# Two row tiles centred instead of normalised at the head of a fused attention and feed-forward kernel, with the first loads in another order

## The chip, the cores and the metric

The kernel runs on one core of a Trainium2 chip. The metric is the device time of one execution in microseconds (us). A core has TensorE (PE, matmuls, with weight loads PEld beside them), VectorE (DVE), ScalarE (ACT), GpSimd (POOL) and SyncE (SP, which here only issues DMAs). Each engine executes its own queue in order; waits between engines go by semaphores. PSUM, which matmuls write, has eight banks.

## The reference

A block on x of 2048 rows and 576 columns: layer norm, then a linear attention and a gated feed-forward in parallel, both added to x.

```python
xn = _layernorm(x)                          # (x - mean) / sqrt(var + 1e-5), per row
# A: 32 heads of 18 columns
q, k, v = split(xn @ wqkv)                  # wqkv: 576 x 1728
phi = lambda t: where(t > 0, t + 1, exp(t)) + 1e-6
kv = einsum("bhsd,bhse->bhde", phi(k), v);  z = einsum("bhsd->bhd", phi(k))
o = einsum("bhqd,bhde->bhqe", phi(q), kv) / (einsum("bhqd,bhd->bhq", phi(q), z)[..., None] + 1e-6)
A = o.reshape(B, S, D) @ wo
# B: F = 4608
B = (gelu(xn @ w_gate) * (xn @ w_up)) @ w_down
return x + A + B
```

All tensors are bf16.

## The kernel before

The 2048 rows are 16 tiles of 128 (`n` = 0 to 15) and four chunks of 512 (`sc`, four tiles each). The feed-forward width is 36 slices of 128 (`f`), loaded two at a time as blocks (`load_gu`): a `wg` and a `wu` tile for the first 512 rows of the weights, and for every second block a `wr` tile with the last 64 rows of both.

**The head**, up to about 58 us, prepares everything that needs all rows. For each tile: `x` is loaded, mean and variance come from two bn_stats and an aggregate on DVE, rstd from Ln and Exp on ACT (`ln_rstd`), and the normalised tile `xn` from DVE or ACT as the string `NORM` says (`ln_norm`, L318). A copy of 64 columns on POOL (`x_twin`) pads the tile to 640 columns, so that its last 64 rows stand twice when transposed. The transposed tile `xnT` comes in two ways: tiles 0 to 3 by ten small transposes on PE into PSUM banks 0 and 1 and two copies (ACT and DVE, `tp_copy`), tiles 4 to 15 by a DMA through the crossbar (`dma_transposes`, L346), which SP issues.

Then come the units on PE. A token unit K*n* or Q*n* multiplies tile *n* with the K or Q columns of `wqkv`; a unit g*f* multiplies the first 512 rows with a slice of gate and up. Each is a `_Unit` (L241): two accumulators in two banks, each fed by matmuls of 64 rows at once. In the first part (`rows`) the lower half of the rows works on the first bank and the upper half on the second; then they take turns, for which POOL gives a sign (`swap`), and the second part (`p2`) follows. A `_Token` unit is either read at once for phi (Exp on ACT, a clamp and a combining operation on DVE) or, for the names in `RAW_T`, copied out by ACT (`raw`, L406) and given its phi after 40 us. A unit can begin only when the former owner of its two banks has been read. K and Q of the head take their banks from one ring (`HEAD_T`), the others from another.

The order of PE is written by hand in `line` (L441): two units are open at a time. `t0` to `t3` are the transposes on PE, "." closes the oldest open unit. All other engines, SP's queue among them, are put in order by a planner (`in_order`, L67): every step has an engine, a cost, a rank, what it comes after and a time before which it is not planned; each engine then executes in the planned order. So the constants `X_AT`, `W_AT` and `DMA_FREE` change the order only, they are not waits. The loads at L189 to L207 stand ahead of the planned ones: x of tiles 0 to 3, K's and Q's weights, x of tiles 4 to 9, and block 0 in between. `first_loads` (L539) fixes the order of those that follow on SP. Each DMA signals one of eight semaphores in turn, and a DMA waits at issue until the one that last used its semaphore has landed.

`z_add` sums phi(K) over the tiles on DVE. After the head, `gram` multiplies phi(K) with `xn` on PE, and the rest is steady: gate and up of the remaining slices, the down product and the outputs, chunk by chunk.

Of the kernel before, what the change touches and what calls it, by code (L numbers as in the profile page):

```python
# [14 lines left out]
P = 128  # L15
HP = 64
# [21 lines left out]
NWARM = 43  # L38
# [7 lines left out]
HEAD_T = RAW_T + ("K2",)  # L46
LATER = 40.0

# [38 lines left out]
def kernel(  # L87
# [32 lines left out]
    banks, head_banks = _Ring([0, 1, 4, 5, 6, 7, 2, 3]), _Ring([4, 5, 6, 7, 2, 3])  # L120
# [31 lines left out]
    xn = apool.tile([P, NS, XW], BF16, name="xn")  # L152
    g_sb = apool.tile([P, KT, D], BF16, name="g_sb")
    z_sum = apool.tile([P, D], F32, name="z_sum")
    z_bf = apool.tile([P, D], BF16, name="z_bf")

# [3 lines left out]
    def load_w_main(which):  # L160
        c = slice(which * D, (which + 1) * D)
        nc.sync.dma_start(wqkv_sb[:, 0:4, c], A_wqkv[0:4 * P, c].rearrange("(kt p) c -> p kt c", p=P))

# [30 lines left out]
    load_x(1, 1, nc.scalar)  # L194
    load_w_main(1)
    load_w_last(1, LO)
    load_w_last(1, HI)
    load_x(2, 1)
    load_w_main(0)
    load_x(3, 1)  # L200
    load_w_last(0, LO)
    load_w_last(0, HI)
    load_x(4, 2)
    load_x(6, 2)
    load_gu(0, 0)
    load_gu(0, 1)
    load_x(8, 2)  # L207

    eps_ln = const.tile([P, 1], F32, name="eps_ln")
# [94 lines left out]

    def ln_aggr(n):
        nc.vector.bn_aggr(out=mv[:, n, :], in_=ln_raw[n][:])
# [11 lines left out]
    def ln_norm(n):  # L318
# [4 lines left out]
        else:  # L323
            nc.vector.tensor_scalar(
                out=xn[:, n, :], in0=x_sb[:, n, :], scalar1=mv[:, n, 0:1], scalar2=rstd[:, n:n + 1],
                op0=ALU.subtract, op1=ALU.mult,
# [9 lines left out]
    def transposes(n):  # L336
        for kt in range(KT):
            for b, rows in enumerate((LO, HI)):
                nc.tensor.transpose(tp_bank(b)[:, kt, :], xn[rows, n, kt * P:(kt + 1) * P], ident[rows, rows])

    def tp_copy(n, b):
        copy = nc.vector.tensor_copy if b else nc.scalar.copy
        t0 = n * P + b * HP
        copy(out=xnT[:, :, t0:t0 + HP], in_=tp_bank(b)[:, 0:KT, :])  # L344
# [4 lines left out]
    X_AT = [3.35, 4.40, 7.10, 9.20]  # L349
    W_AT = {"K": 6.00, "Q": 8.80}  # L350
    DMA_FREE = 12.7
# [5 lines left out]
    for n, at in ((4, 10.2), (6, 11.2), (8, 14.5)):  # L357
        step(("x", n), "none", 0.0, 0, [], lambda: None, ready=at)
    for n in range(10, NS, 2):
        load(("x", n), 0.58, 295, 7.0 + 2.5 * (n - 10), [], lambda n=n: load_x(n, 2), ready=6.0)  # L360

    for n in range(NS):
# [3 lines left out]
        x_at = X_AT[n] if n < 4 else 11.5 if n < 8 else 2.1 * both  # L366
        if n < 4:
            step(("twin", n), "POOL", 0.2, first, [], lambda n=n: x_twin(n, 1), ready=x_at)
        elif n == both:
            step(("twin", n), "POOL", 0.25, first, after_x, lambda n=n: x_twin(n, 2), ready=2.6 * n)  # L370
        twin = ("twin", n if n < 4 else both)
        for h in range(2):
            step(("stats", n, h), "DVE", 0.42, first, after_x, lambda n=n, h=h: ln_half(n, h), ready=5.1 if (n, h) == (1, 1) else x_at)
        step(("aggr", n), "DVE", 0.16, first, [("stats", n, 0), ("stats", n, 1)], lambda n=n: ln_aggr(n), tail=0.05)
        if n < 6:
            step(("rstd", n), "ACT", 0.46, first - 2.0 * (n == 3), [("aggr", n)], lambda n=n: ln_rstd(n, 1))
        elif n == both:
            step(("rstd", n), "ACT", 0.46, first, [("aggr", n), ("aggr", n + 1)], lambda n=n: ln_rstd(n, 2))
# [5 lines left out]
        if n < HEAD:  # L384
            step(("norm", n), on, took, first, ready, lambda n=n: ln_norm(n), tail=0.05)
            free = [("xnT", n - 1, i) for i in range(2)] if n else []
            step(("tp", n), "PE", 0.2, 0, [("norm", n)] + free, lambda n=n: transposes(n), tail=0.15)
            for i, copied in enumerate((0.44, 0.30)):
                step(("xnT", n, i), "DVE" if i else "ACT", copied, first, [("tp", n)], lambda n=n, i=i: tp_copy(n, i), tail=0.02)
            steps[("xnT", n)] = _Step("none", 0.0, first, [("xnT", n, 0), ("xnT", n, 1)], lambda: None, 0.0, 0.0)  # L390
        else:
# [3 lines left out]
    class _Token:  # L395

        def __init__(self, kind, n, ring=banks):
# [3 lines left out]
                [ps_all[:, b, :HALF] for b in self.banks], lambda i, rows, kt: xnT[rows, kt, n * P:(n + 1) * P],  # L401
                lambda i, rows, kt: wqkv_sb[rows, kt, self.c + i * HALF:self.c + (i + 1) * HALF], nc.gpsimd, first=range(KT),
            )
            self.acc = ps_all[:, self.banks[0]:self.banks[0] + 2, :HALF]

# [526 lines left out]
```

## Time and profile before

| | us |
|---|---|
| median of 3 runs (range) | 509.65 (509.18 to 510.46) |
| profiled execution | 509.63 |
| its span, first to last instruction | 507.8 |
| first K matmul (K0) | 6.60 |
| first g matmul (g0) | 14.04 |
| first matmul of `gram` | 58.25 |
| granted PE clock, all slices | 0.9 or more |

PE is busy in 99% of the span. The profile's page, its waits, its timeline and the chain of waits are all of this one execution; times in them start at the span's start. In a timeline row the columns are start, length, engine, line, operation, tiles written and read, form, count, and in brackets the engine's idle time just ahead and what ended it. A DMA row gives queue, count, size and the median time from issue to landing.

### The profile page before, as it was taken

The numbers are of one execution on the slowest core, as the hardware profiler recorded it, in microseconds if no ns is written. First come the engines' busy times: TensorE is split into PE (matmuls) and PEld (weight loads), VectorE is DVE, ScalarE is ACT, GpSimd is POOL, SyncE is SP. The second block draws the span as 40 slices with busy tenths as digits, with TensorE's granted clock in tenths as the row PEclk, the third lists the DMA queues.
The fourth block names the chain that finished last, engine by engine and source line by source line (L and its number), as shares of the span: only waits on it lengthen the run. The fifth ranks groups of instructions, "written<-read, shape, count | busy, mean of one in ns | idle before, by whom it ended". The sixth has DMA issues, their size and how long they took to land.

```text
span 507.8 us, 11198 instructions
## 1 busy us (share of the span) xinstructions
PE 502.7 (99%) x4772; PEld 305.6 (60%) x4772; DVE 228.7 (45%) x477; ACT 151.9 (30%) x265; POOL 8.2 (2%) x32
## 2 busy tenths in 40 slices
PE   8999999999999999999999999999999999999997
PEld 7566875446777444445777444445777444445774
DVE  5778966774101665543101665543101665543101
ACT  4888634335000532233000432233000432232000
POOL 2110000000000000000000000000000000000000
PEclk9999999999999999999999999999999999999999
DMA  9999906996200555654000455654000555640000
GB/s 263 239 220 241 266 1 180 248 269 121 71 13 25 145 150 156 176 163 108 12 13 25 142 151 152 179 162 109 14 12 26 144 151 156 175 112 14 13 13 23
DMA packets 113611, 61.58 MB, mean 121 GB/s; under 512 B 23250, under 2 KB 113562, under 8 KB 113562
## 3 DMA queue, kind: packets, MB, share of 16 engines
q1 hardware_dynamic: 113418, 60.72, 46.9%
q8 instruction: 37, 0.61, 0.5%
q10 hardware_dynamic: 144, 0.15, 0.1%
q14 instruction: 12, 0.10, 0.1%
HBM read 53.75 MB, written 2.36 MB: 110 GB/s over the span
## 4 chain that ended last, share of the span: by engine, by line
PE 94%; DVE 3%; DMA 2%; SPq 1%; issue 0%; ACT 0%; DVEq 0%
PE ps_all L252 58%; PE ps_all L847 28%; PE ps_all L558 3%; PE ps_all L852 3%; DVE hT L422 1%; DMA wu<-in_B_w_up_dram 1%; DMA wqkv_sb<-in_A_wqkv_dram 1%; DVE z_sum L529 1%; DVE phi_e L416 0%; PE ps_all L835 0%; PE ps_all L566 0%; DVE pq L422 0%; SPq L158 0%; PE ps_all L585 0%; PE ps_all L787 0%
## 5 line engine op out<-in xcount | busy, mean ns | idle before, releaser
L252 PE MATMUL ps_all<-xnT,wu 64*128 64x512 bf16 x1152 | 272.7, 376 | 0.3 <-DMA wu<-in_B_w_up_dram 0.3
L252 PE MATMUL ps_all<-xnT,wg 64*128 64x512 bf16 x1152 | 272.6, 376 | 0.0
L252 PEld LDWEIGHTS <-wu 64*128 64x128 bf16 x1152 | 107.9, 94 | 68.4 <-DMA wu<-in_B_w_up_dram 0.8
L252 PEld LDWEIGHTS <-wg 64*128 64x128 bf16 x1152 | 108.2, 94 | 65.2
L740 DVE TENSOR_TENSOR hT<-ps_all,gl 128x512 bf16<-128x512 f32 x130 | 89.9, 691 | 104.1 <-ACT gl L739 104.0
L847 PEld LDWEIGHTS <-hT 128*128 128x128 bf16 x1152 | 110.8, 98 | 30.9 <-issue 1.2
L739 ACT ACTIVATE gl<-ps_all 128x512 f32<-128x512 f32 x130 | 77.6, 597 | 164.1 <-PE ps_all L252 163.7
L861 DVE TENSOR_TENSOR res<-ps_all,x_sb 128x288 bf16<-128x288 f32 (+2 forms) x32 | 13.8, 455 | 146.3 <-PE ps_all L852 88.1
L847 PE MATMUL ps_all<-wd_a,hT 128*128 128x288 bf16 (+2 forms) x512 | 68.3, 286 | 0.0
L252 PE MATMUL ps_all<-xnT,wr 64*128 64x512 bf16 x288 | 57.3, 376 | 0.0
L847 PE MATMUL ps_all<-hT 128*128 128x288 bf16 (+2 forms) x384 | 52.4, 286 | 0.0
L761 ACT ACTIVATE gl<-ps_all 128x288 f32<-128x288 f32 x24 | 9.2, 410 | 121.4 <-PE ps_all L252 118.5
L847 PE MATMUL ps_all<-wd_m,hT 128*128 128x288 bf16 (+2 forms) x256 | 36.8, 286 | 0.0
L252 PEld LDWEIGHTS <-xnT 64*128 64x128 bf16 x576 | 32.6, 94 | 6.7 <-ACT xnT L344 0.9
L252 PE MATMUL ps_all<-wqkv_sb,xnT 64*128 64x288 bf16 x360 | 27.8, 283 | 0.7 <-ACT xnT L344 0.3
L252 PEld LDWEIGHTS <-wr 64*128 64x128 bf16 x288 | 15.2, 94 | 16.4
L852 PE MATMUL ps_all<-m_sb,pqT 128*128 128x288 bf16 (+2 forms) x128 | 20.9, 286 | 0.0
L558 PE MATMUL ps_all<-hT,xn 128*128 128x288 bf16 x128 | 16.0, 286 | 0.0
L437 ACT CAST hT<-ps_all 128x1024 bf16<-128x1024 f32 x14 | 14.1, 1010 | 4.0 <-PE ps_all L252 3.8
L558 PEld LDWEIGHTS <-xn 128*128 128x128 bf16 x128 | 12.4, 98 | 3.5 <-issue 0.5
L852 PEld LDWEIGHTS <-pqT 128*128 128x128 bf16 x128 | 12.4, 98 | 3.3
L303 DVE BATCH_NORM_STATS2 stats<-x_sb 128x6 f32<-128x288 bf16 x32 | 12.9, 435 | 2.9 <-DMA x_sb<-in_A_x_dram 2.9
(79 smaller groups left out, 228.4 us busy)
## 6 DMA issues: line engine op xcount, KB each, us to landing
wg<-in_B_w_gate_dram SPq DMA_DIRECT2D x72, 256.0 KB, 3.0
wu<-in_B_w_up_dram SPq DMA_DIRECT2D x72, 256.0 KB, 3.7
wr<-in_B_w_gate_dram SPq DMA_DIRECT2D x36, 64.0 KB, 3.2
wr<-in_B_w_up_dram SPq DMA_DIRECT2D x36, 64.0 KB, 2.9
wd_a<-in_B_w_down_dram SPq DMA_DIRECT2D x4, 576.0 KB, 8.2
out_dram<-res SPq DMA_DIRECT2D x15, 144.0 KB, 1.8
wqkv_sb<-in_A_wqkv_dram SPq DMA_DIRECT2D x3, 576.0 KB, 5.6
x_sb<-in_A_x_dram SPq DMA_DIRECT2D x6, 288.0 KB, 4.3
```

The source lines that it names most:

```text
L252: return nc.tensor.matmul(self.outs[i], lhsT=self.lhs(i, rows, kt), rhs=self.rhs(i, rows, kt), start=start, stop=stop, skip_group_check=True,)
L303: nc.vector.bn_stats(out=ln_raw[n][:, h, :], in_=x_sb[:, n, h * HALF:(h + 1) * HALF])
L422: nc.vector.scalar_tensor_tensor(out=dst[:, self.n, :].rearrange("p (h c) -> p h c", h=2), in0=self.acc, scalar=0.0, in1=self.e[:].rearran ...
L437: nc.scalar.copy(out=hT[:, self.f:self.f + NF + 1:NF, :], in_=ps_all[:, self.two[0]:self.two[0] + 2, :],)
L529: nc.vector.tensor_tensor(out=(z_bf if i == NS - 1 else z_sum)[:], in0=pk[:, z_order[0], :] if i == 1 else z_sum[:], in1=pk[:, z_order[i], :],
L558: nc.tensor.matmul(ps_all[:, two[hf], :HALF], lhsT=xn[:, n, kt * P:(kt + 1) * P], rhs=pk[:, n, hf * HALF:(hf + 1) * HALF], start=(n == 0), ...
L739: nc.scalar.activation(out=gl[:], in_=ps_all[:, b[0], :], func=ACT.Gelu_apprx_tanh)
L740: nc.vector.tensor_tensor(out=hT[:, GUB * k + i, :], in0=ps_all[:, b[1], :], in1=gl[:], op=ALU.mult)
L761: nc.scalar.activation(out=e[:, :HALF], in_=acc, func=ACT.Exp)
L847: nc.tensor.matmul(self.acc(hf), lhsT=hT[:, f, j * P:(j + 1) * P], rhs=wd(f)[:, self.parts[hf]], start=(f == 0 and not paired), stop=False ...
L852: nc.tensor.matmul(self.acc(hf), lhsT=pqT[:, c, self.ts], rhs=m_sb[:, c, self.parts[hf]], start=False, stop=(paired and c == 3), skip_grou ...
L861: nc.vector.tensor_tensor(out=self.res[:, hs], in0=self.acc(hf), in1=x_sb[:, self.n, hs], op=ALU.add)
```

## The change

For tiles 0 and 1 (`CENTRED`), K and Q are computed from the centred tile, x minus mean, and rstd is applied where the unit's result is copied out of PSUM: per row, on ACT for tile 0 and on DVE for tile 1. The tile normalised in full is made later, and its transpose for the g units comes by a crossbar DMA (`xnU`). The statistics of tile 1 are a sum on ACT, a mean on POOL and a squared sum on ACT. rstd of tiles 1 and 2 is one pair of instructions. The transposes of tiles 0, 1 and 2 use different columns of their banks.

Of the loads: Q's main weights come in four quarters (64 rows by 288 columns of each of four blocks), the last 64 rows of K's and of Q's weights as one DMA each into a tile `w_ends`, K's on ACT's queue. Block 0 of gate and up stands right behind x of tile 3; x of tiles 4 to 9 is planned behind it. Q2 moves from the end of `line` to its head, the warm-up on PE is 36 matmuls for 43, and the ring of banks has another order.

```diff
-NWARM = 43
+NWARM = 36
-HEAD_T = RAW_T + ("K2",)
+HEAD_T = RAW_T + ("K2", "Q2")
+CENTRED = (0, 1)
...
-    banks, head_banks = _Ring([0, 1, 4, 5, 6, 7, 2, 3]), _Ring([4, 5, 6, 7, 2, 3])
+    banks, head_banks = _Ring([0, 1, 6, 7, 4, 5, 2, 3]), _Ring([4, 5, 6, 7, 2, 3])
...
+    def load_w_quarters(which, halves):
+        for rows, half in zip((LO, HI), halves):
+            c = which * D + half * HALF
+            view = A_wqkv[0:4 * P, c:c + HALF].rearrange("(kt p) c -> p kt c", p=P)
+            nc.sync.dma_start(wqkv_sb[rows, 0:4, c:c + HALF], view[rows])
+    def load_w_ends(which, on=nc.sync):
+        c = which * D
+        on.dma_start(w_ends[:, which, :], A_wqkv[512:576, c:c + D].rearrange("r (i c) -> i r c", i=2))
...
     load_x(1, 1, nc.scalar)
+    load_w_ends(1, nc.scalar)
     load_w_main(1)
-    load_w_last(1, LO)
-    load_w_last(1, HI)
     load_x(2, 1)
-    load_w_main(0)
+    load_w_quarters(0, (0, 1))
+    load_w_quarters(0, (1, 0))
+    load_w_ends(0)
     load_x(3, 1)
-    load_w_last(0, LO)
-    load_w_last(0, HI)
-    load_x(4, 2)
-    load_x(6, 2)
     load_gu(0, 0)
     load_gu(0, 1)
-    load_x(8, 2)
...
+    def act_sum(n):
+        nc.scalar.activation(out=act_junk[:], in_=x_sb[:, n, 0:D], func=ACT.Copy, accum_out=act_acc[:])
+    def act_mean(n):
+        for out, by in ((mv[:, n, 0:1], 1.0), (act_bias, D ** -0.5)):
+            nc.gpsimd.tensor_scalar(out=out[:], in0=act_acc[:], scalar1=-by / D, scalar2=None, op0=ALU.mult)
+    def act_square(n):
+        nc.scalar.activation(
+            out=act_junk[:], in_=x_sb[:, n, 0:D], func=ACT.Square, bias=act_bias[:], scale=D ** -0.5, accum_out=mv[:, n, 1:2],
+        )
+    def centre(n):
+        nc.vector.tensor_scalar(
+            out=xn[:, n, :], in0=x_sb[:, n, :], scalar1=mv[:, n, 0:1], scalar2=None, op0=ALU.add if n else ALU.subtract,
+        )
...
-        copy(out=xnT[:, :, t0:t0 + HP], in_=tp_bank(b)[:, 0:KT, :])
+        copy(out=(xcT if n in CENTRED else xnT)[:, :, t0:t0 + HP], in_=tp_bank(b)[:, at:at + KT, :])
...
-    for n in range(10, NS, 2):
+    for n in range(4, NS, 2):
         load(("x", n), 0.58, 295, 7.0 + 2.5 * (n - 10), [], lambda n=n: load_x(n, 2), ready=6.0)
...
+            if late:
+                load(("xnU", n), 1.25, 80, first + 2, [("norm", n)], lambda n=n: dma_transposes(n))
...
-            nc.scalar.copy(out=dst, in_=self.acc)
+            if self.n == 0:
+                nc.scalar.activation(out=dst, in_=self.acc, func=ACT.Identity, scale=rstd[:, 0:1])
+            elif self.n == 1:
+                nc.vector.tensor_scalar(out=dst, in0=self.acc, scalar1=rstd[:, self.n:self.n + 1], scalar2=None, op0=ALU.mult)
+            else:
+                nc.scalar.copy(out=dst, in_=self.acc)
...
-    line = ["t0", "K0", "t1", ".", "K1", "Q0", "t2", "Q1", "t3", "K2", "K3", "g0", "g1", "g2", "g3"]
+    line = ["t0", "t1", "K0", "K1", "Q0", "t2", "Q1", "K2", "Q2", "t3", ".", "K3", "g0", "g1", "g2", "g3"]
...
-    line += ["Q2", "Q3"]
+    line += ["Q3"]
...
-            after = [("xnT", m) for m in range(TPC)] + ([("gu", blk, i) for i in range(2)] if blk else [])
+            after = [("xnU" if m in CENTRED else "xnT", m) for m in range(TPC)] + ([("gu", blk, i) for i in range(2)] if blk else [])
...
+        of += [("phi", "K13")] * (i == 8)
...
     first_loads = [
-        ("x", 10), ("xnT", 4), ("gu", 2, 0), ("xnT", 5), ("gu", 2, 1), ("x", 12), ("xnT", 6), ("x", 14), ("xnT", 7),
-        ("gu", 3, 0), ("gu", 3, 1), ("gu", 4, 0),
+        ("xnU", 0), ("x", 4), ("xnU", 1), ("x", 6), ("gu", 1, 0), ("gu", 1, 1), ("x", 8), ("x", 10), ("xnT", 4), ("gu", 2, 0), ("xnT", 5), ("gu", 2, 1), ("x", 12), ("gu", 3, 0), ("xnT", 6), ("gu", 3, 1), ("xnT", 7), ("x", 14), ("gu", 4, 0),
     ]
```

## The prediction

> **What bounds the kernel now.** I read the page first, then who waited for whom on PE, then the chain of waits, then PE's timeline where the chain leaves PE. The page settles the scale: PE is the bound, and only waits that PE meets can be won.
>
> ```profile
> PE 502.7 (99%) x4772; PEld 305.6 (60%) x4772; DVE 228.7 (45%) x477; ACT 151.9 (30%) x265; POOL 8.2 (2%) x32
> PE 94%; DVE 3%; DMA 2%; SPq 1%; issue 0%; ACT 0%; DVEq 0%
> ```
>
> The second line is the chain's share by engine: some 25 of 507.8 us belong to something other than PE, and the chain in order of time says where.
>
> ```profile
> 1.26 4.65 DMA wqkv_sb<-in_A_wqkv_dram
> ...
> 9.38 5.49 DMA wu<-in_B_w_up_dram
> 14.86 0.04 issue
> 14.91 25.64 PE ps_all L252 x271
> ...
> 54.64 0.77 DVE hT L422
> 55.41 0.04 issue
> 55.45 2.87 PE ps_all L252 x44
> ```
>
> Columns are start, length, what. K's weights land at 5.91 (1.26 + 4.65), the first `wu` block at 14.86, and phi of K13 on DVE ends at 55.41; PE continues right after the last two. From 14.91 to 53.9 PE has no gap (38.94 of 38.94 us busy in that window), and after 58 it runs from `gram` on. So the change can win in two places, which PE's timeline shows:
>
> ```profile
> 6.60 0.79 PE L252 MATMUL ps_all<-wqkv_sb,xnT 64*128 64x288 bf16 x10 [0.26 <-ACT xnT L344]
> ...
> 14.04 0.40 PE L252 MATMUL ps_all<-xnT,wr 64*128 64x512 bf16 x2
> 14.26 0.38 PE L252 MATMUL ps_all<-xnT,wg 64*128 64x512 bf16 x1
> 14.91 0.39 PE L252 MATMUL ps_all<-xnT,wu 64*128 64x512 bf16 x1 [0.27 <-DMA wu<-in_B_w_up_dram]
> ...
> 53.87 1.42 PE L252 MATMUL ps_all<-wqkv_sb,xnT 64*128 64x288 bf16 x18
> 55.45 2.87 PE L252 MATMUL ps_all<-wqkv_sb,xnT 64*128 64x288 bf16 x44 [0.16 <-DVE hT L422]
> ```
>
> Work in these units: two 512-wide matmuls of a pair of row halves start 0.216 us apart, so a g unit (9 pairs) is 1.94; a K and a g follow each other every 3.045 (24.44, 27.49, 30.53 in the timeline), so a token unit is 1.105 (its first five pairs 0.61, its last four 0.49). g0 starts at 14.04, but its second `wu` matmul runs at 14.91 where 14.26 was due: 0.65 lost, as if g0 had begun at 14.69. At the tail 53.87 + 1.105 = 54.98, and PE goes on at 55.45: 0.47 lost to phi of K13.
>
> **The change part by part.**
>
> *Start.* Without rstd on the way, `centre` of tile 0 follows its aggregate (4.42): 4.45 to 4.90, by the 0.45 of the norm at 5.08. Transposes come 0.2 later, 5.1 for 5.74, and the warm-up is cut to suit: 7 of 43 matmuls at 4.75/43 = 0.11 each, 0.77, so it ends at 5.05. ACT's copy (0.43, row at 6.09) ends at 5.86. In the built program the transposes of tile 1 still wait for both copies of tile 0, though they use other columns of the banks, so t1 goes at 5.9 and K0 at 6.1. There K's weights bind: 5.91 before, and `w_ends` (72 KB, on ACT's queue) comes in beside them, about 0.2: K0 at 6.18 against 6.60.
>
> *Tile 1.* Its sum on ACT replaces two bn_stats (0.82) and an aggregate (0.21) on DVE. No row has an ACT operation with accumulation; an exp of 576 is 0.65, a norm of 640 is 0.91, I take 0.65 (end 4.45; the upper end 4.7 is still ahead of the copy of tile 0, so nothing moves). POOL's mean is 2 x 0.27 by the nbias row, its twin copies and the turns of the banks queue behind it for 0.5 us, when no turn is due yet. ACT's square (0.65 to 0.95) lies between 6.7 and 7.7, ahead of rstd of tile 2, whose aggregate comes at 7.6 (x2 at 6.5 for 6.71): covered to 0.1.
>
> *From K0 to g0.* K0, K1, Q0, Q1, K2, Q2 are six units, 6.63, t2 and t3 0.16 each, K3's first part 0.61: 7.56, so 13.74 with no wait. Waits on the way: (a) Q's last rows come by one DMA behind the quarters on SP, and its semaphore is the one of K's weights, so SP holds it and all behind it until 6.15; before, SP stood at the same place until 5.93. Q0 wants it at 8.39. An x tile in an empty queue took 2.53, the four 72 KB weight rows 4.2 in the median: 8.7 to 10.3. I take 8.7, as only 280 KB are ahead: 0.35, at worst 1.9. (b) raw K1 is now on DVE, between the norm of tile 1 and the copy of tile 2: 0.76 by the phi row, 0.45 by the norm row; I take 0.76, and K2 waits 0.07. (c) rstd of tile 3 waits behind raw Q0 on ACT, t3 0.04 late. (d) raw Q1 stands ahead of the copy of tile 3 on DVE, which ends at 13.83: K3 waits 0.28. Together 0.74: PE is ready for g0 at 14.48. Q2 is in it, which before was in the tail.
>
> *The new wait of g0.* It no longer waits for `wu` but for xnT of tiles 0 and 1, which the crossbar now writes. SP issues every 0.57 us (5.93 to 9.93 before, 8 starts), so with `wqkv` last rows at 6.15, x3, two wr, wg and wu follow, the transpose of tile 0 stands at 9.55, x4 at 10.8, the transpose of tile 1 at 11.4 (a transpose holds SP 1.2).
>
> ```profile
> xnT<-xn SPq DMA_TRANSPOSE x2, 4.7
> ...
> pqT<-pn SPq DMA_TRANSPOSE x7, 3.4
> ...
> wg<-in_B_w_gate_dram SPq DMA_DIRECT2D x72, 256.0 KB, 3.0
> wu<-in_B_w_up_dram SPq DMA_DIRECT2D x72, 256.0 KB, 3.7
> ```
>
> The last column is the time from issue to landing: 4.7 for crossbar transposes in the crowded head, 3.4 in mid run. The queue is less full here (x4, x6 and x8 are behind, not ahead), so 3.4: 14.8, g0 at 14.85, a wait of 0.35. With 2.65 (the shortest, at 231.0) it would be none, with 4.7 it is 1.65. wg and wu, issued by 9.0, are in by 12.7 (3.7) and hide behind it.
> The Trainium skill, page Advanced Engine Details and Errata, section X-Bar Transpose (TRN2), holds crossbar transposes to be as fast as regular DMAs. By that page the transpose of tile 1 would land like an x tile, at 13.9, and the sum would be 0.35 better; the rows above say otherwise, and I go by them.
> *Quarters.* Total bytes are as before; the first two quarters land near 7.5, ahead of Q0 at 7.90. As one load they would all come at about 8.5, and 0.6 would be lost.
> The Trainium skill, DMA: Bandwidth & Descriptors, section Rules for kernel authors, advises against two transfers to partition halves, since both use the same engines one after the other. Here that order is the point; by the page the gain is nought and the sum 0.6 worse, if PE could not use the first half alone.
>
> *What is late next.* x4, x6 and x8 were ahead of g0's weights and are now behind them: x4 lands at 14.0 (10.8 + 3.2, between 2.5 for an x alone and 4.3 for 288 KB rows of the head) where it came at 10.35. On DVE its stats stand ahead of phi of K2, which frees g1's banks: 14.0 + 0.82 + 0.23 + 0.29 + 0.76 = 16.15; g1 is due at 14.85 + 1.08 + 0.49 = 16.42, cover 0.27. Behind that phi on DVE: norm of tile 4 to 16.6, stats and aggregate of tile 5 to 17.65. SP waits for that norm, issues the transpose (16.65, 13.89 before; landed 4.7 later at 21.35, K4 due 22.3), two wr, wg. Tile 5's rstd (0.55), bias on POOL (0.3) and norm on ACT (0.92) end at 19.5; its transpose goes at 19.65 and `wu` of block 2, queued behind it, at 20.9, 18.69 before. Due at 23.58 + (14.85 - 14.47) = 23.96, where 14.47 is when g0's gate half could go on before. By 3.0 it lands at 23.9, by 3.7 at 24.6, by the 4.37 of its own row in the head at 25.3. I take 3.0, no wait, and keep 1.35 for the range. Block 1's `wu` at 13.8 + 3.7 = 17.5 is due at 18.4.
>
> *Tail.* Q2 is gone, and its bank's place is Q3's; the fourth z add of that stretch now comes after phi of K13. Three z adds (2.33 from 51.98) stood ahead of it, now one phi and one z (1.8): 0.5 earlier, so the 0.47 goes; if DVE is later there, none of it.
>
> *Sum.* g0 14.85 against 14.69: +0.16. Q2 done: -1.105. Tail: -0.47. Total -1.4: span 507.8 to 506.4. The profiled run took 509.63, 1.83 around its span, and the median of the runs is 509.65; the forecast is 508.2.
>
> **The rivals.** *No new wait at all*: transposes in 2.65 and Q's last rows in time: g0 at 14.1, -2.15, 507.5. For it, the mid-run row; against it, the crowded head. *Given back*: transpose 4.7 (g0 16.15), then block 2's `wu` within that shift: +1.46 - 1.58 = -0.1, 509.5. For it, the two rows at 4.7. *Slower*: the x4 path decides. By the updates of their semaphores a transpose of the head took up to 6.5 us (issued at 13.89) and the x load ahead of it 5.9 (12.46 to 18.38). With x4 at 16.7, norm 4, both transposes and `wu` of block 2 all come 2.7 later: 23.6 + 4.37 = 28.0, due 23.96, a wait of 4.0: -1.4 + 4.0 = +2.6, 512.2. It turns slower than before once that `wu` lands after 25.4, and beyond the bound after 26.9. Against it: the queue ahead of 12.46 was full, here SP has little outstanding. That the change does not do what it says touches 0.42 us at most: K0 moves from 6.60 to 6.18, since K's weights bind from there, and the rest of the gain is Q2's place and the tail.
>
> **How the numbers follow.** About 0.3% (1.5 us) is what a measurement of this kernel can tell from no change, so 508.1 is the border to faster, and the forecast stands on it. Forecast 0.66, its own range 507.5 to 509.2, half on each side of 508.1; no new wait 0.10; given back 0.08; slower 0.16. Faster 0.33 + 0.10 = 0.43, same 0.33 + 0.08 = 0.41, slower 0.16. Range 507.3 to 510.6: below, all waits gone; above, half of the slower case.
>
> **What would show it.** K0's first matmul at 6.2 (6.60); g0 at 14.7 to 15.0, ended by the transpose and not by `wu`; the x4 stats at 14; no gap at the first matmul of block 2 (`wu`, near 24); no gap between K14 and Q3; `gram` at 56.9 for 58.3. Wrong: g0 beyond 16, a gap ahead of g1 (DVE) or at block 2 over 1 us, a wait of Q0 over 1 us, or PE's clock below full after the shorter warm-up.

## The result, and the profile after

| | median us (from to, runs) | profiled run, its span | K0 | g0 | `gram` |
|---|---|---|---|---|---|
| before | 509.62 (509.18 to 510.46, 4) | 509.63, 507.8 | 6.60 | 14.04 | 58.25 |
| after | 514.03 (513.59 to 514.90, 4) | 513.59, 511.8 | 5.96 | 18.11 | 62.50 |

The changed kernel is slower: after over before is 1.0087, with a 95% interval of 1.0067 to 1.0106. The last three columns are starts on PE's timeline. K0 is 0.64 us earlier, as the change is to make it, and g0 is 4.07 later; from g0 to `gram` both kernels need about the same (44.21 before, 44.39 after), and after `gram` the spans differ by 0.25. From K0 to g0 it takes 12.15 us for 7.44, of which 1.1 is Q2, now in the head. The equal stretches behind g0 hide a second loss: the changed kernel has Q2's 1.1 and the tail's 0.47 less to do there, and loses as much again before `gram`.

The page of the changed kernel first: the line of busy times, and the chain's share by engine.

```profile
PE 502.4 (98%) x4765; PEld 304.6 (60%) x4765; DVE 230.2 (45%) x478; ACT 152.4 (30%) x265; POOL 8.9 (2%) x34
...
PE 96%; DMA 3%; ACT 0%; issue 0%; SPq 0%; DVE 0%
```

PE does the same work (502.4 for 502.7), but DVE, which held 3% of the chain before, is gone from it, and DMA has 3%. The chain in order of time (start, length, what) says which transfers these are.

```profile
1.27 4.65 DMA wqkv_sb<-in_A_wqkv_dram
5.92 0.02 issue
5.93 6.29 DMA w_ends<-in_A_wqkv_dram
12.23 0.04 issue
12.27 0.79 PE ps_all L265 x10
...
24.86 4.51 DMA wu<-in_B_w_up_dram
29.38 0.05 issue
29.43 33.15 PE ps_all L265 x380
```

Q's last rows, 72 KB, are issued at 5.93, when K's weights have landed, and take 6.29 us. Later the `wu` of block 2 is issued at 24.86 and takes 4.5. The last line is new on the good side: from 29.43 to `gram` at 62.57 PE has no gap, so the tail's wait for phi of K13 is gone. PE's timeline shows each wait.

```profile
5.96 0.67 PE L265 MATMUL ps_all<-wqkv_sb,xcT 64*128 64x288 bf16 x8
9.46 0.30 PE L265 MATMUL ps_all<-w_ends,xcT 64*128 64x288 bf16 x2 [2.83 <-DMA w_ends<-in_A_wqkv_dram]
...
12.27 0.30 PE L265 MATMUL ps_all<-w_ends,xcT 64*128 64x288 bf16 x2 [0.92 <-DMA w_ends<-in_A_wqkv_dram]
...
18.11 0.39 PE L265 MATMUL ps_all<-xnT,wr 64*128 64x512 bf16 x2
...
27.93 0.39 PE L265 MATMUL ps_all<-xnT,wg 64*128 64x512 bf16 x1 [0.40 <-DMA wg<-in_B_w_gate_dram]
...
29.43 0.39 PE L265 MATMUL ps_all<-xnT,wu 64*128 64x512 bf16 x1 [1.11 <-DMA wu<-in_B_w_up_dram]
```

K0's first four pairs run at 5.96, and its fifth, the one that reads `w_ends`, stands 2.83 for it. Q0's fifth pair stands 0.92. Block 2 stands 0.40 and 1.11. These four are 5.26 us of waiting. The kernel before has five waits from its first transposes to `gram`, none over 0.3 and together 1.08.

Why a DMA of 72 KB takes 6 to 8 us is seen in the DMA engines (the changed kernel first, then the kernel before). The columns that matter are the last two, the mean busy share of the 16 DMA engines and GB/s:

```profile
8.00:9.00 1.00, 0.00 (x0) 0.00 (x0) 0.74 (x2) 0.00 (x0) 0.24 (x1) 1.00 0.55 108
9.00:10.00 1.00, 0.54 (x10) 0.51 (x11) 0.29 (x2) 0.50 (x2) 0.00 (x0) 1.00 0.34 108
10.00:11.00 1.00, 1.00 (x21) 0.93 (x18) 0.80 (x2) 0.10 (x1) 0.00 (x0) 1.00 0.33 88
11.00:12.00 1.00, 0.35 (x6) 0.14 (x3) 0.00 (x0) 0.64 (x1) 0.00 (x0) 1.00 0.44 127
```

```profile
8.00:12.00 4.00, 3.77 (x76) 2.89 (x74) 3.13 (x11) 2.79 (x9) 0.53 (x2) 1.00 1.09 290
```

For four microseconds a third to a half of the engines is busy, in the stretch in which the kernel before moved 290 GB/s. The semaphore updates in the trace tell which. "Median" is the ninth of 16 updates, or the second of three. Every other load of the head raises its semaphore 16 times as it lands; a `w_ends` load raises it 3 times, once at its start and twice late:

```
                 issued   first   median   last     updates
w_ends K           1.49    2.72     9.02    9.42     3
w_ends Q           5.93    6.98    12.01   12.23     3
x2                 1.73    5.64     6.10    8.24    16
Q, 1st quarter     2.28    6.48     6.85    9.22    16
Q, 4th quarter     4.38    8.43     8.79   10.71    16
x3                 6.62    9.40     9.64   12.55    16
```

The load is written with the half of the columns outermost (`r (i c) -> i r c`, i = 2), and its two late updates say that the data runs on two of the sixteen engines. Whatever comes behind it has its share on those two engines as well: of Q's fourth quarter fourteen updates are there by 9.07 and two come at 10.67 and 10.71; of x3 fourteen by 9.85 and two at 12.39 and 12.55. In the kernel before all updates of x2 lie between 6.06 and 6.71. The Trainium skill states the rule (DMA: Bandwidth & Descriptors, section "Why a DMA increments its semaphore by 16 and not by 1"): such a DMA uses the largest number of engines up to 16 that divides the slowest dimension of both sides, only these post an update, and the issuing sequencer writes the rest at once. Three updates, one of them early, are what it makes of a dimension of 2, and this trace agrees. What it does to the loads queued behind is in the table.

The late load also held SP, since a DMA waits at issue until the one that last used its semaphore has landed. The view of SP's own waits up to 20 us has this row:

```profile
SPq L195 <- DMA w_ends<-in_A_wqkv_dram: 1.5, 1, 1.5
```

Block 0's first `wr` load uses the semaphore of K's `w_ends`. SP issued nothing from 7.91 until that had landed at 9.42, so part of the idle share between 8 and 12 is an emptier queue. The runs below do not separate the two effects: without the two-engine load both are gone.

### The profile page after: what moved, and what is told of

Same layout as the page of the kernel before. It is cut to its first block, busy times and chain, and to the rows that moved or that the text cites. A ratio compares the mean times of both kernels' runs of the same rounds, so it can differ in the third digit from the quotient of the medians.

```text
span 511.8 us, 11194 instructions
## 1 busy us (share of the span) xinstructions
PE 502.4 (98%) x4765; PEld 304.6 (60%) x4765; DVE 230.2 (45%) x478; ACT 152.4 (30%) x265; POOL 8.9 (2%) x34
## 4 chain that ended last, share of the span: by engine, by line
PE 96%; DMA 3%; ACT 0%; issue 0%; SPq 0%; DVE 0%
PE ps_all L265 61%; PE ps_all L901 28%; PE ps_all L612 3%; PE ps_all L906 3%; DMA w_ends<-in_A_wqkv_dram 1%; DMA wqkv_sb<-in_A_wqkv_dram 1%; DMA wu<-in_B_w_up_dram 1%; PE ps_all L889 0%; PE ps_all L620 0%; PE ps_all L639 0%; ACT hT L489 0%; PE ps_all L841 0%; SPq L162 0%; DVE res L915 0%; PE ps_all L369 0%
## 5 line engine op out<-in xcount | busy, mean ns | idle before, releaser
L265 PEld LDWEIGHTS <-xnT 64*128 64x128 bf16 x504 | 28.4, 94 | 6.1 <-DMA xnT<-xn 0.5
L265 PE MATMUL ps_all<-wqkv_sb,xnT 64*128 64x288 bf16 x256 | 21.2, 283 | 0.0
L906 PE MATMUL ps_all<-m_sb,pqT 128*128 128x288 bf16 (+2 forms) x128 | 20.9, 286 | 0.0
L612 PEld LDWEIGHTS <-xn 128*128 128x128 bf16 x128 | 12.4, 98 | 3.5 <-issue 0.5
L906 PEld LDWEIGHTS <-pqT 128*128 128x128 bf16 x128 | 12.4, 98 | 3.3
```

Of the source, the lines that this page charges most:

```text
L265: return nc.tensor.matmul(self.outs[i], lhsT=self.lhs(i, rows, kt), rhs=self.rhs(i, rows, kt), start=start, stop=stop, skip_group_check=True,)
L612: nc.tensor.matmul(ps_all[:, two[hf], :HALF], lhsT=xn[:, n, kt * P:(kt + 1) * P], rhs=pk[:, n, hf * HALF:(hf + 1) * HALF], start=(n == 0), ...
L906: nc.tensor.matmul(self.acc(hf), lhsT=pqT[:, c, self.ts], rhs=m_sb[:, c, self.parts[hf]], start=False, stop=(paired and c == 3), skip_grou ...
```

## The experiments

All times are medians; "diff" is the run's median less that of the kernel before, timed beside it on the same chip. The interval is that of the ratio.

| run | built on | median | diff | ratio, 95% interval |
|---|---|---|---|---|
| after | | 514.03 | +4.41 | 1.0087 [1.0067, 1.0106] |
| e1_ends_two | after | 512.09 | +2.47 | 1.0045 [1.0032, 1.0058] |
| e2_before_ends_one | before | 511.05 | +1.43 | 1.0029 [1.0020, 1.0038] |
| e3_ends_joint | after | 512.09 | +2.39 | 1.0043 [1.0028, 1.0058] |
| e4_x4_first | e3 | 511.14 | +1.44 | 1.0031 [1.0019, 1.0043] |
| e5_tail_alone | before | 509.48 | -0.22 | 0.9997 [0.9989, 1.0006] |
| e6_q3_in_head | e4 | 513.73 | +4.12 | 1.0083 [1.0070, 1.0097] |
| e7_no_centring | e4 | 509.91 | +0.30 | 1.0010 [1.0000, 1.0020] |
| e8_crossbar_early | e4 | 511.10 | +1.41 | 1.0024 [1.0015, 1.0033] |
| e9_x14_early | e4 | 511.31 | +1.62 | 1.0029 [1.0019, 1.0039] |
| e10_q2_and_tail | before | 508.95 | -0.62 | 0.9990 [0.9981, 0.9999] |
| e11_idle_crossbars | e7 | 510.46 | +0.89 | 1.0015 [1.0006, 1.0024] |
| e12_quarters_alone | e10 | 510.90 | +1.30 | 1.0040 [1.0019, 1.0062] |
| e13_joint_ends | e10 | 508.49 | -1.11 | 0.9977 [0.9968, 0.9987] |

### The two-engine load undone: e1_ends_two

```diff
-        on.dma_start(w_ends[:, which, :], A_wqkv[512:576, c:c + D].rearrange("r (i c) -> i r c", i=2))
+        for i, rows in enumerate((LO, HI)):
+            on.dma_start(w_ends[rows, which, :], A_wqkv[512:576, c + i * HALF:c + (i + 1) * HALF])
```

> The changed kernel, but the last 64 rows of K's and of Q's weights come as two DMAs of 64 rows by 288 columns each in place of one DMA with an outer dimension of two. Theory A (the one DMA runs on two of the 16 DMA engines, 64 rows on each, and holds up everything behind it on those two): the last rows land by 7 (K) and 9 (Q), the waits of K0 (2.8) and of Q0 (0.9) go, x of tile 2 lands near 6.6 for 8.24; 508 to 510 us. Rival B (the crossbar transposes and x4 behind block 0 set the pace): the time of the changed kernel to within 1 us, 513 to 515, with g0 at 18 as now. Rival C (the semaphore that holds SP until K's weights have landed): no change of SP's starts, since the added DMAs hold it there as well, or earlier; 513 to 515.

512.09. K's last rows land at 6.00 and 6.71 with 16 updates each, x2 at 6.42 (8.24), and K0 runs through. So the two-engine load, with the hold of SP that it brings, costs 1.9 of the 4.4. It is not the whole, as the waits of PE up to 80 us show (total, times, longest):

```profile
PE ps_all L266 <- DMA w_ends<-in_A_wqkv_dram: 1.7, 2, 0.9
PE ps_all L266 <- DMA wu<-in_B_w_up_dram: 1.2, 1, 1.2
...
PE ps_all L266 <- DMA xnT<-xn: 0.8, 1, 0.8
```

Q's last rows are still late (issued at 6.39 and 7.05, behind the fourth quarter, which SP holds until K's weights land at 5.74), and Q0's fifth pair waits for them, 1.7 in two pieces; g0 waits for the crossbar transpose of tile 1, and block 2 for its `wu`.

### The two-engine load put into the kernel before: e2_before_ends_one

```diff
+        on.dma_start(w_ends[:, which, :], A_wqkv[512:576, c:c + D].rearrange("r (i c) -> i r c", i=2))
-    load_w_last(1, LO)
-    load_w_last(1, HI)
+    load_w_ends(1)
...
-    load_w_last(0, LO)
-    load_w_last(0, HI)
+    load_w_ends(0)
```

> The kernel before with one part of the change alone: the last 64 rows of K's and of Q's weights each as one DMA with an outer dimension of two, on SP, into a tile of their own. Theory A: 64 rows on each of two engines, some 2 to 4 us of those engines each time; K0's fifth pair of matmuls waits until 8 or later and x of tile 2 is as late; 512 to 514 us. Rivals B and C (the cost is in the crossbar transposes, in x4, or in SP's wait): 509 to 510.3, as before.

511.05, +1.43: the direction as expected, the size short of it. K's last rows landed at 7.47, and K0 did not wait for them as was expected. Q's landed at 11.76, and Q0's fifth pair waited 1.5 for them. x2 had its last two updates late again (7.50 and 7.82, against 6.71 in the kernel before), and `gram` came at 59.71. The edit also takes two issues off SP, which may be why the size is short; no run shows it. Put in and taken out, the load costs 1.4 and 1.9.

### The last rows joined on ACT's queue: e3_ends_joint

```diff
+        ends = A_wqkv[512:576, 0:2 * D].rearrange("r (w i c) -> i r w c", w=2, i=2)
+        for i, rows in enumerate((LO, HI)):
+            on.dma_start(w_ends[rows, :, :], ends[i])
...
-    load_w_ends(1, nc.scalar)
+    load_w_ends(nc.scalar)
...
-    load_w_ends(0)
```

> The changed kernel, with K's and Q's last rows together in two DMAs of 64 rows x 2 x 288 (one for each half of the partitions), both issued on ACT's queue ahead of K's weights; nothing of them is left on SP. In the run with two DMAs for each (512.09) Q0's fifth pair still waited 1.7, since SP was held until K's weights had landed (5.75) before the fourth quarter, and Q's last rows were issued behind it at 6.39 and 7.05. Theory A (Q's last rows are late because of their place in SP's queue, and all of SP behind them with them): Q0's wait for w_ends is gone, SP is some 1.3 ahead, the crossbar transposes of tiles 0 and 1 are issued by 10.6 and 12.6, g0 starts at 15.7 to 16.2 rather than 17.27, and the run takes 510.7 to 511.2. Rival B (the transposes wait for their own normalised tiles or for late DMA engines, not for SP): Q0's wait is gone and g0 is still at 17.0 to 17.4, waiting for xnT; 511.8 to 512.2. Rival C (36 KB of Q's rows ahead of K's weights cost what they save): K0 at 6.4 or later.

512.09 in the median of six executions that fall in two groups: 510.90 to 511.25, about where theory A put the time, and 512.92 to 513.07. The profile is of the slowest. In it theory A is right up to g0 (no wait for `w_ends`, transposes issued at 9.38 and 11.97, g0 at 15.28 after a wait of 0.71 for a transpose), and what g0 gained comes back behind it, as waits of 2.1 and 0.4 for `wu` of blocks 1 and 2 and 1.3 for DVE. One of the sixteen engines brought block 1's `wu` some 3 us after the others (fifteen updates by 18.55, PE released at 21.45). That this is what parts the two groups is likely, not shown.

### x4 to x7 ahead of block 0 again: e4_x4_first

```diff
     load_x(3, 1)
+    load_x(4, 2)
+    load_x(6, 2)
     load_gu(0, 0)
...
-        ("xnU", 0), ("x", 4), ("xnU", 1), ("x", 6), ("gu", 1, 0), ...
+        ("xnU", 0), ("xnU", 1), ("gu", 1, 0), ...
```

> As the run with the last rows joined, and x4 to x7 ahead of block 0's gate and up again, as the kernel before had them (x8 stays behind block 1's). Theory A (the order of gate/up ahead of x4 makes block 2's wu late by way of x4, norm 4 and 5 and their transposes on SP): the wait for block 2's wu (1.1 in the changed kernel, 1.2 in the run with two DMAs each) goes, g0 is not later than in the run with the last rows joined because block 0's weights would land by about 15.5, and the time is about 1.0 to 1.2 below that run. Rival B (g0 then waits for block 0's weights): a wait of 0.5 to 1.5 at g0 for wg or wu, and the time is as that run's or up to 0.5 above.

511.14, 0.95 below the median of e3. No `wu` is waited for any more; g0 waits instead:

```profile
PE ps_all L267 <- DMA xnT<-xn: 1.7, 1, 1.7
...
PE ps_all L267 <- DVE hT L478: 0.7, 1, 0.7
```

g0 starts at 16.34 and waits 1.74 for the transpose of tile 1 (issued 12.28, landed 16.21): neither theory had that, the weights of block 0 were in. The executions (510.81 to 511.74) are no faster than the faster group of e3, and the intervals overlap: what gate and up ahead of x4 cost, 0.95 by the medians, is not resolved.

### The tail alone: e5_tail_alone

```diff
+        of += [("phi", "K13")] * (i == 8)
         step(("z", i), "DVE", 0.76, 80.0, ...)
```

> The kernel before with one edit of the change alone: z(8) waits until phi of K13 is done, so that three additions to z_sum no longer stand ahead of the last tokens' phi on DVE. If that is what emptied the tail, the gaps ahead of the gram (in the kernel before two stretches in which PE waits for DVE's hT, 0.47 together) go and the time is 0.3 to 0.5 lower, 509.1 to 509.35, ratio about 0.9992. If the gap only moves to Q3 or to the later additions, the time is within 0.15 of the kernel before.

-0.22, not to be told from zero. The waits of the tail are gone from the profile, but in this execution g0 came 0.82 later (Q's last rows landed at 10.18), so `gram` stands at 58.21 for 58.25. The run does not decide what the tail is worth.

### Q3 in the head: e6_q3_in_head

```diff
-HEAD_T = RAW_T + ("K2", "Q2")
+HEAD_T = RAW_T + ("K2", "Q2", "Q3")
...
-    line = [..., "t3", ".", "K3", "g0", ...]
+    line = [..., "t3", ".", "K3", "Q3", "g0", ...]
```

> As the run with x4 to x7 ahead of block 0 again (511.14), and Q3 as well moved from the tail to the head, between K3 and g0. In that run PE was through with the head's chains at about 14.6 and stood 1.74 until the crossbar transpose of tile 1 had landed (issued 12.28, landed 16.21, g0 at 16.34). Theory A (g0's start is set by the crossbar alone, and the wait is time that other work can fill): g0 stays at 16.2 to 16.5, its wait falls to 0.5 to 0.8, one chain of 1.1 is gone from the tail, the gram starts at 58.8 to 59.2 rather than 59.95 and the time is 510.0 to 510.4. Rival B (Q2 and Q3 were the cover of the last tokens' phi): g0 the same, and the gram waits for DVE by as much as the head gained; 510.9 to 511.3.

513.73, worse by 2.6 than e4, and for a reason that neither theory had. g0 stood at 16.84, without a wait, after 1.05 ahead of Q3 for K2's phi; then g1 waited 3.03 for the phi of Q3, whose banks it takes. Behind it the granted clock fell (the third last column):

```profile
20.00:21.00 1.00, 0.00 (x0) 0.00 (x0) 0.86 (x3) 0.57 (x4) 0.35 (x2) 0.97 1.29 67
21.00:22.00 1.00, 0.38 (x2) 0.13 (x3) 0.96 (x3) 1.00 (x2) 0.38 (x2) 0.50 0.81 190
22.00:23.00 1.00, 1.00 (x8) 0.48 (x6) 0.97 (x4) 0.68 (x1) 0.00 (x0) 0.50 1.19 254
23.00:24.00 1.00, 1.00 (x8) 0.37 (x5) 1.00 (x4) 0.50 (x2) 0.00 (x0) 0.50 1.28 285
```

So work that fills a gap of PE gains nothing if it keeps the banks that the next unit needs.

### Without the centring: e7_no_centring

```diff
-CENTRED = (0, 1)
+CENTRED = ()
...
-            if self.n == 0:
-                nc.scalar.activation(out=dst, in_=self.acc, func=ACT.Identity, scale=rstd[:, 0:1])
-            elif self.n == 1:
-                nc.vector.tensor_scalar(out=dst, ...)
-            else:
-                nc.scalar.copy(out=dst, in_=self.acc)
+            nc.scalar.copy(out=dst, in_=self.acc)
...
-    line = ["t0", "t1", "K0", "K1", "Q0", ...]
+    line = ["t0", "K0", "t1", ".", "K1", "Q0", ...]
...
-        ("xnU", 0), ("xnU", 1), ("gu", 1, 0), ...
+        ("gu", 1, 0), ...
```

> As the run with x4 to x7 ahead of block 0 again (511.14), without the centring: tiles 0 and 1 are normalised at once as in the kernel before, transposed by PE into the shared tile alone, no crossbar transpose ahead of tile 4's, the raw copies are plain copies on ACT. Kept of the change: Q's weights in quarters, the last rows in a tile of their own (in two DMAs), Q2 in the head, the banks, the tail. Theory A (what is left of the loss is the crossbar): no wait for xnT at g0, which starts when PE is through with the head's chains, 14.9 to 15.5 with Q2 among them; gram at 58.0 to 58.5; 509.3 to 509.9, so the centring costs 1.2 to 1.8 here. Rival B (the loss lies in the head's chains, the quarters or the joined last rows): g0 at 16.0 or later without a wait for xnT; 510.6 to 511.3.

509.91, by the differences 1.14 below e4, near the 1.2 to 1.8 that theory A gave; its place was wrong, and there rival B was right (g0 at 16.0 or later, without a wait for a transpose). g0 starts at 16.61, later than with the centring (16.34), for the normalised tile 1 holds t1 by 0.56 and the last rows hold K0 by 0.39; part of that is this execution's, in which K's weights landed at 6.35 (5.64 in e4). The gain comes behind g0: no wait up to `gram` at 58.73 (59.88 in e4). So the centring does start K0 sooner, and with these loads the transposes it needs take that back and more.

### Two orders of SP's queue: e8_crossbar_early, e9_x14_early

```diff
 e9: -        ("x", 12), ("gu", 3, 0), ("xnT", 6), ("gu", 3, 1), ("xnT", 7), ("x", 14), ("gu", 4, 0),
     +        ("x", 12), ("x", 14), ("gu", 3, 0), ("xnT", 6), ("gu", 3, 1), ("xnT", 7), ("gu", 4, 0),
 e8, besides:
     -        ("xnU", 0), ("xnU", 1), ("gu", 1, 0), ...
     +        ("xnU", 0), ("gu", 0, 0), ("xnU", 1), ("gu", 0, 1), ("x", 6), ("gu", 1, 0), ...
```

> As the run with x4 to x7 ahead of block 0 again (511.14), with SP's queue ordered by what PE needs: after x3 come x4 and x5, then the crossbar transpose of tile 0, block 0's wr and gate, the transpose of tile 1, block 0's up, x6 and on; and x14 directly behind x12 rather than behind block 3 and tiles 6 and 7. The centring stays. In the run it builds on, the transposes were issued at 10.38 and 12.28 behind 0.85 MB of loads and landed at 15.44 and 16.21, PE waited 1.74 for them, and x14 (issued 27.98, landed 32.6) held DVE and so PE for 0.7. Theory A (the loss that is left is those two orders on SP, not the centring itself): transposes issued by 8.5 and 11, landed by 14; g0 at 14.7 to 15.2; no wait for hT; gram at 57.3 to 58.3; 508.0 to 509.3, below the kernel before. Rival B (the loads that are moved back cost as much): g0 waits for block 0's up until 16 or later, or tile 4 comes too late by way of x6 and x4; 510.5 to 511.5.

> As the run with x4 to x7 ahead of block 0 again (511.14), and x14 directly behind x12 on SP; nothing else. Theory A: the wait of 0.7 for hT at 34.2 goes (x14 lands by about 28 rather than 32.6), g0 stays at 16.2 to 16.5 with its wait of 1.7 for the crossbar, gram at 58.8 to 59.3, 510.2 to 510.6. Rival B (DVE's lateness there has another cause): the wait for hT stays, 511.0 to 511.3.

511.10 and 511.31: neither gained on e4 (511.14). In e9 the wait for hT went, as theory A said, and another came at 43.6, 0.64 for a transpose. In e8 g0 started at 15.28 after 0.52 of waiting for a transpose, and block 0's `wu` was waited for 0.91, as rival B said. The transpose of tile 0 was issued at 7.82, 2.6 earlier, and landed at 13.33, 5.5 later. The windows of e8 show what the DMA engines did:

```profile
10.00:11.00 1.00, 1.00 (x18) 0.70 (x15) 1.00 (x3) 0.30 (x2) 0.00 (x0) 1.00 3.21 145
11.00:12.00 1.00, 1.00 (x18) 0.93 (x19) 0.70 (x3) 0.94 (x2) 0.00 (x0) 1.00 0.05 6
12.00:13.00 1.00, 1.00 (x21) 0.92 (x18) 0.61 (x2) 0.27 (x2) 0.03 (x1) 1.00 0.77 184
```

Between 11 and 12 all DMA engines together move 6 GB/s. Some twenty packets of 256 B of the transpose, begun between 10.2 and 10.8, last 1.6 to 2.2 us and all end at 12.4 (the share of 3.21 is their time, booked where they begin), while one engine fetches 16 KB of instructions (10.40, 0.96 us) and works off what had queued there. x4, issued ahead of it at 7.26, landed at 12.65. So with a transpose in flight, and one engine late, all the others stood too; that the transpose is the reason is a reading of this one stretch. Its earlier place gained nothing.

### Two edits of the change alone: e10_q2_and_tail

```diff
-HEAD_T = RAW_T + ("K2",)
+HEAD_T = RAW_T + ("K2", "Q2")
...
-    banks = _Ring([0, 1, 4, 5, 6, 7, 2, 3])
+    banks = _Ring([0, 1, 6, 7, 4, 5, 2, 3])
...
-    line = [..., "t3", "K2", "K3", "g0", ...] ... ["Q2", "Q3"]
+    line = [..., "t3", "K2", "Q2", "K3", "g0", ...] ... ["Q3"]
...
+        of += [("phi", "K13")] * (i == 8)
```

> The kernel before with two of the change's edits alone: Q2 in the head ahead of K3 (with the change's order of the banks), and z(8) held until phi of K13 is done. No centring, no quarters, no tile for the last rows, gate and up behind x4 as before. Theory A (the two are worth what the prediction said where nothing else of the change is in the way: PE works on Q2 while it would wait for block 0's up, 0.27, and the tail's waits of 0.2 to 0.47 go): g0 at 15.0 to 15.6, no wait for wu there, gram at 57.5 to 58.0, 509.0 to 509.4. Rival B (they are worth nothing: the head's chains wait for Q's last rows and tile 3 instead): 509.5 to 509.9.

508.95, faster than the kernel before by 0.62, with an interval that just leaves out no change. g0 at 15.12, no wait for `wu`, `gram` at 57.25: from g13 (the last gate and up) to `gram` it takes 5.85 where the kernel before takes 7.42, that is Q2's 1.1 and 0.47.

### The transposes without a reader: e11_idle_crossbars

```diff
+            if n < 2:
+                load(("xnU", n), 1.25, 80, first + 2, [("norm", n)], lambda n=n: idle_transposes(n))
...
-        ("gu", 1, 0), ("gu", 1, 1), ...
+        ("xnU", 0), ("xnU", 1), ("gu", 1, 0), ("gu", 1, 1), ...
```

> The run without the centring (509.91), with the two crossbar transposes of tiles 0 and 1 put back at their place on SP, behind block 0's up, but into a tile that nothing reads: gate and up read PE's own transposes. So no instruction waits for them, and what they cost is only what they take from SP (1.2 each) and from the DMA engines. Theory A (a crossbar transpose holds all DMA engines until the last of them has arrived, so the loads behind it come 1 to 2 later and a part of the 1.2 that the centring cost is theirs alone): block 1's and x8's loads land 1.5 to 2.5 later than in the run without, a wait for wu, hT or xnT of 0.5 to 1.2 after g0, and 510.4 to 511.1. Rival B (what cost was g0's own wait for them): no new wait after g0, 509.8 to 510.2.

510.46, 0.55 above e7, with intervals that overlap. The loads behind came later as expected (block 1's `wu` 18.70 for 17.65, x8 20.21 for 18.45, x10 21.85 for 19.25), yet no wait of theory A's size shows after g0, and in the profiled run the granted clock was 0.50 to 0.74 between 8 and 12, where e7's was 1.00. That the transposes cost something without a reader is likely, not shown.

### Which of the load edits costs: e12_quarters_alone, e13_joint_ends

```diff
 e12: -    load_w_main(0)
      +    load_w_quarters(0, (0, 1))
      +    load_w_quarters(0, (1, 0))
 e13: -    load_w_main(1)
      -    load_w_last(1, LO)
      -    load_w_last(1, HI)
      +    load_w_ends(nc.scalar)
      +    load_w_main(1)
      ...
      -    load_w_last(0, LO)
      -    load_w_last(0, HI)
```

> The kernel before with Q2 in the head and the tail's edit (508.95), and Q's weights in quarters; the last rows as the kernel before loads them (two DMAs for each of K and Q on SP), no centring. Theory A (every DMA that is added ahead costs, as SP issues it and then waits for a semaphore that an earlier one still holds: three more issues of 0.6 to 0.8 and a wait until K's weights land at 5.6 to 5.9): Q's last rows are issued 1 to 2 later than in the run without and Q0 or Q1 waits for them 0.5 to 1.0; 509.6 to 510.2. Rival B (the quarters let Q0 begin before all of Q has landed, and this pays): 508.5 to 508.9.

> The kernel before with Q2 in the head and the tail's edit (508.95), and K's and Q's last rows in a tile of their own, loaded together in two DMAs of 64 rows x 2 x 288 on ACT's queue; Q's weights in one DMA, no centring. Theory A (fewer issues on SP and Q's last rows early: nothing behind them waits): SP two issues ahead, K0 at 6.5 to 6.8, 508.6 to 509.1. Rival B (the 72 KB ahead of K's weights and x2 hold K0 or tile 2): K0 or its fifth pair waits 0.4 to 0.7 for w_ends, 509.3 to 509.9.

510.90 and 508.49 against 508.95 for the kernel both are built on: the quarters cost 1.95, the joined last rows save 0.46 (for the latter the intervals overlap). The executions of e12 spread from 510.12 to 513.96; its fastest is 1.4 above the fastest of e10, so the price lies between 1.4 (by the fastest) and 1.95 (by the medians). In e12 Q's last rows are issued at 7.94 and 8.47 rather than 4.62, and tile 3 and block 0 behind them. About 1 us of that is the profiled execution's, in which K's weights, whose semaphore the fourth quarter waits for, landed at 6.64 (5.58 in e10). But the waits for issue are not all. From 6 to 8 us the kernel before, e12, and e13 moved this (last two columns: share, GB/s):

```profile
6.00:8.00 2.00, 1.58 (x40) 1.05 (x34) 1.41 (x5) 0.93 (x4) 0.24 (x1) 1.00 1.09 351
```

```profile
6.00:8.00 2.00, 1.32 (x30) 0.80 (x24) 0.88 (x4) 1.02 (x4) 0.03 (x1) 1.00 1.02 206
```

```profile
6.00:8.00 2.00, 1.99 (x42) 1.31 (x38) 1.35 (x5) 0.82 (x3) 0.24 (x1) 1.00 1.07 322
```

The engines are as busy in all three and move 206 GB/s with the quarters, 351 and 322 without (227 in e4, 196 in e7). Half a row is 576 B, and a packet of 576 B took 45 ns there in e12 where one of 1152 B took 57 in the kernel before: half the data for four fifths of the time. Length alone is not it: packets of 512 B (`wg`, `wu`) took 33 ns in the kernel before, where it moved 281 to 309 GB/s. Why 576 B are slower than 512 B stays open, and so does what taking half of the rows at a time adds, which the quarters do as well. e13 has the lowest median of all kernels here, 1.1 us (0.23%, interval 0.13 to 0.32) below the kernel before and 5.5 below the changed one. Its chain of waits and its waits up to 60 us:

```profile
PE 99%; DVE 0%; ACT 0%; issue 0%; DVEq 0%
```

```profile
PE ps_all L233 <- DVE x_sb L199: 1.1, 1, 1.1
PE ps_all L255 <- DVE mv L309: 0.2, 1, 0.2
```

The 1.1 is the start of the warm-up, and 0.2 is left.

### The account

By medians, each against the kernel before beside it: after +4.41; less the two-engine load, +2.47; less the place of the last rows, +2.39; less gate and up ahead of x4, +1.44; less the centring, +0.30; less the quarters (e13, rebuilt on the kernel before), -1.11. The parts are 1.94, 0.08, 0.95, 1.14 and 1.41. By the intervals each is uncertain by 0.7 to 1.2, so the second and third are not resolved, and each holds in that order only. The last step changes more than the quarters (the warm-up is 43 matmuls again, and t3, x8 and others stand elsewhere); what the quarters cost by themselves is e12's number. The first part and the quarters are shown by a second run (1.43 in e2, 1.4 to 1.95 in e12). Whether the centring would pay with Q in one load, where the transposes queue behind faster loads, no run here measured, and it stays open.

## Why the prediction was wrong

*The step that failed.* "`w_ends` (72 KB, on ACT's queue) comes in beside them, about 0.2", and term (a), Q's last rows at 8.7, "0.35, at worst 1.9". Both were priced by bytes, beside the four 72 KB loads of the kernel before, which run on sixteen engines. K's last rows landed at 9.42 and not 6.1, Q's at 12.23 and not 8.7. K0 started as forecast (5.96 for 6.18) and stood 2.83 at its fifth pair, a wait the sum did not have; Q0 stood 0.92, from a start already 2.8 late. Before the fifth pair K0 reads only K's main weights, which were in at 5.92. The forecast also had no term for SP, which the same load held for 1.5 ahead of block 0. e1, which changes the form of that load alone, takes 1.94 of 4.41 away.

*Quarters.* "Total bytes are as before" is true, and "as one load they would all come at about 8.5, and 0.6 would be lost" had the arrival right (8.51 in e13) and the price wrong: Q0 there starts without a wait for it. What was missed is that these half rows move at about 0.6 of the rate (206 GB/s against 351 and 322), so that x3, tile 3 and everything behind come later. The rule of the Trainium skill that the prediction weighed there and set aside, against transfers to partition halves, had the right sign; e12 prices it, with the half rows that come with it here, at 1.4 to 1.95.

*What is late next.* "By 3.0 it lands at 23.9 ... I take 3.0, no wait, and keep 1.35 for the range": `wu` of block 2 was issued at 24.86 and took 4.5. The row for it in the head of the kernel before was 4.37, and over the whole run `wu`'s own row says 3.7; the 3.0 is the row of `wg`. The issue was forecast at 20.9, so 4.0 of the lateness is the late issue and 1.5 the longer landing. With `wg`'s 0.40 the wait was 1.51. One sum of that passage is off by 0.05 (14.0 + 0.82 + 0.23 + 0.29 + 0.76 is 16.10, not 16.15); nothing hangs on it. The rival that was named slower had this place right, x4 behind block 0, and a price (4.0) that the run did not reach; by e4 that order is worth 0.95 in the medians, unresolved.

*The new wait of g0.* The transposes took 3.43 each (12.59 to 16.02, 14.64 to 18.07), the 3.4 of the sum. g0 came at 18.11 since the issue was 3.2 later than forecast, behind the late rows. PE reached it without a visible wait only because it was as late itself; in e4, with the head repaired, the wait is 1.74, not 0.35.

*Tail and Q2.* Forecast -0.47 and -1.105; from g13 to `gram` it takes 6.09 for 7.42, -1.33 of 1.58, and -1.57 in e10. These steps were right by the profiles and by e10, in which the two edits together make a kernel that is 0.62 faster; the tail alone was not resolved (e5).

*Start.* The gain at K0's start was forecast at 0.42 and was 0.64. The edits that buy it touch every load of the head. The forecast's chance of slower, 0.16, rested on one mechanism (x4) and held none for a load that is slow by its form.

## What to carry to other kernels

Ahead of a DMA-bound start, price a load by its access pattern before its bytes: the outermost dimension says how many engines it runs on, and the form of its rows how fast each goes (in this head whole rows of 1152 B and rows of 512 B moved well, half rows of 576 B did not). Here one load of Q beat four quarters that should have let PE begin earlier. Ask too what else waits for the load's semaphore: here it was SP, and with it all loads behind. When a profile shows a small transfer that takes long, count the updates of its semaphore and compare the median with the last engine of the loads behind it. And try the parts of a change one by one on the kernel before: here Q2's place and the tail were a gain together (e10), hidden under the rest.

## What the runs showed of the hardware

- A load on two of sixteen engines delays those behind it on these two: x2 6.10 in the median, 8.24 at the last (6.34 and 6.71 before); of Q's fourth quarter fourteen updates by 9.07, two at 10.67 and 10.71.
- Rows of 576 B moved at 196 to 227 GB/s with all engines busy, rows of 1152 B at 322 to 351. The Trainium skill (DMA: Bandwidth & Descriptors, section Specifications) puts the least transfer for line rate at 512 B. Rows of 512 B did well here (33 ns a packet, 281 to 309 GB/s in the kernel before); for 576 B, which is above that least, this case does not agree, and the measurement decides.
- With a crossbar transpose in flight and one engine late, all DMA engines together moved 6 GB/s for a microsecond (e8, 11 to 12), and packets of 256 B took up to 2.2 us.
- SP waits before it issues a load whose semaphore an earlier load still holds: the fourth quarter in e1 was issued at 5.75, when K's weights had landed at 5.74, 2.0 after the third.
- After 3.03 us without a matmul the granted clock was 0.50 for 3.4 us (e6, from 20.93); a gap of 2.83 in the changed kernel (6.63 to 9.46) brought no fall. A long gap is not the only way to it: in e11 it was 0.50 from 8.10 for 3.4 us after gaps of at most 0.63 from 3.7 on. What sets it stays open.
- A sum by ACT's accumulation is two instructions, 0.68 and 0.19 for the read of the accumulator; the prediction had one of 0.65.
